# Slots 11 to 20 of a top-k attention and feed-forward kernel under one written timetable

## The chip, the cores and the metric

The kernel runs on one core of a Trainium2 chip. The metric is the device time of one execution in microseconds. Before the change the median of three runs is 1386.3 us (1385.4 to 1386.99).

## The reference

Queries, keys and values have 8 batches, 8 heads, 576 rows and a head dimension of 64. Each row of scores keeps its 32 largest entries, and the softmax over them weights the values. The heads of a row laid side by side give x (4608 rows of 512), which goes through a feed-forward block without biases.

```python
scores = scale * np.matmul(q, k.transpose(0, 1, 3, 2))
kth = np.partition(scores, -top_k, axis=-1)[..., -top_k:-top_k + 1]
scores = np.where(scores >= kth, scores, -1000000000.0)
attn = softmax(scores); x = rows of np.matmul(attn, v), heads side by side
h = x @ w_in
g = h * (1.0 / (1.0 + np.exp(-1.702 * h)))
return (g @ w_out).astype(np.float32)
```

All data are float32.

## The kernel before

The attention is cut into 144 slots, 18 to a batch. A slot holds 128 rows of scores for each of two heads: four tiles of 128 rows for each of four head pairs, and two slots for the last 64 rows of the batch, which pack two pairs each. The order on every engine is written out by hand (a manual schedule): each engine runs its queue in that order, and semaphores set by the tile framework hold an instruction until its operands and its buffer are ready.

A slot n goes through these steps. TensorE multiplies queries and keys (`scores`, L319, called two slots ahead) into one score tile of four PSUM banks. ScalarE copies it to SBUF (`copy_scores`, L334). VectorE pairs the two halves of a row into maxima and minima (`pair_up`, L343, done for slot n+1 within the search of slot n) and finds the 32 largest in four rounds of eight with `MAX8` and `MATCH_REPLACE8` (`topk`, L363; `find`, L1040, interleaves pairing, search and the inversion of the denominators of slot n-1). GpSimd makes the threshold and the shift (`bounds`, L388: `cut`, `low`). ScalarE masks (`mask`, L403) and takes exponentials with their sum (`exps`, L411); together they are `exponentials` (L397). GpSimd adds a small constant to the sum (`some`) and VectorE inverts it (`invert`, L422, `rden`). GpSimd multiplies (`normalize`, L439), ScalarE splits the float32 words into 16-bit halves (`split`, L475), SyncE writes them to DRAM and fetches them transposed (`turn_by_dma`, L483) into one of two `pt` buffers. TensorE multiplies them with the values (`values_at`, L537, for two slots at a time), and ScalarE brings the result into x (`x_of`, L595).

Four slots give one block of 128 rows of x. A block has four hidden units (`hidden`, L635: 16 or 32 matmuls with `w_in` into a PSUM bank), each followed by `tanh` on ScalarE, `gate` on GpSimd (L669), and a projection with `w_out` (`project`, L732). The first two blocks (`whole`) project straight. Later blocks use a product of seven quarter-size parts in place of eight: `combine` (L686) makes sums of the gated parts, and four sums of quarters of `w_out`, t1 to t4, are made once on GpSimd (`weight_sums`, L718, sixteen instructions run by `sum_weights`). Two PSUM banks, `both_banks` (L116, one tile), hold projections and, before slot 11, hidden units; after that, hidden units use the two rotating banks `ps_t`, which also hold q,k turns and attention outputs. When a block is done, `leave` or `leave_parts` copies its bank or banks out, and the parts are merged and written.

Slots 0 to 10 also round the weights and turn the attention by TensorE. Slots 11 and 12 are `first_pair` (L1055), slots 13 to 20 four calls of `filling_pair` (L1089), and from slot 21 `steady_pair` (L1149) runs to the end. The q,k pairs of batch 1 are turned by TensorE (`prepare_by_pe`, L297) at slots 13 to 15, batches 2 on by DMA (`prepare_by_dma`, L263; that of pair (2,0) at slot 21). In `filling_pair(n)` the values of slots n-3 and n-2 are taken late in slot n, between the scores of n+2 and n+3.

A loop serves two slots at once in the pairs, so one written order stands for both. In `first_pair` the output copies of the first block stand inside the second slot's exponentials:

```python
exponentials(n, leave_all)
```

Of the kernel before, what the change touches and what calls it, by code (L numbers as in the profile page):

```python
# [19 lines left out]
P = 128  # L20
# [13 lines left out]
def kernel(  # L34
# [81 lines left out]
    both_banks = ps_p.tile([P, 2, 512], F32, name="po")  # L116
# [53 lines left out]
    def stay_warm(count, of=ident[:]):  # L170

        none = both_banks[:, 1, :]
        for i in range(count):
            nc.tensor.matmul(none[:, 0:P], lhsT=of, rhs=of, start=True, stop=True)
# [122 lines left out]
    def prepare_by_pe(b, hp):  # L297
        for name in "qk":
            prepare_main(name, b, hp)
        second_part.append((b, hp))  # L300

    second_part = []
# [331 lines left out]

    def hidden(into=None):  # L635
        if not ready:
            return
        x = ready[0]
        fs, x.left = x.left[:G], x.left[G:]
        ph = ps_t.tile([P, G * P], F32, name="ph", tag="tp")[:] if into else both_banks[:, 0, :]  # L640
        for i, f in enumerate(fs):
            for c in range(CC):
                parts = 1 if x.whole else 2
                for y in range(parts):
                    rows = slice(y * P // parts, (y + 1) * P // parts)
                    nc.tensor.matmul(  # L646
                        ph[rows, i * P : (i + 1) * P],
                        lhsT=win[:, c, f * P + rows.start : f * P + rows.stop],
                        rhs=xs[:, x.place, c, :],
                        start=(c == 0),  # L650
                        stop=(c == CC - 1),
                    )
        to_gate.append((ph, fs, x))
        if not x.left:
            free.append(ready.pop(0).place)
# [62 lines left out]
    def weight_sums(to, x, y):  # L718

        def part(i, j):  # L720
            of = lambda name: half(name, i)[:, 2 * j : 2 * j + 2, :, :]
            nc.gpsimd.tensor_tensor(out=of(to), in0=of(x), in1=of(y), op=ALU.subtract)

        return [lambda i=i, j=j: part(i, j) for i in range(2) for j in range(2)]

# [6 lines left out]
    def project(put_off_leaving=False):  # L732

        g, sums, fs, x = to_project.pop(0)
        if x.whole:
            for i, f in enumerate(fs):
                nc.tensor.matmul(
                    both_banks[:, 1, :], lhsT=g[:, i * P : (i + 1) * P], rhs=wout[:, f, :],
                    start=(x.done == 0), stop=(x.done == FC - 1),
                )  # L740
                x.done += 1
        else:
            a11, a12, a22, s1, s2, s3, s4 = sums
# [4 lines left out]
            for bank, products in enumerate(banks):  # L748
                for i in range(2):
                    for r, (to, a, w) in enumerate(products):  # L750
                        for y in range(2):
                            nc.tensor.matmul(  # L752
                                both_banks[y * TAIL : (y + 1) * TAIL, bank, to * P : (to + 1) * P],
# [7 lines left out]
        def leave():  # L761
            ob = thp.tile([P, C], F32, name="ob", tag="th")
            nc.scalar.mul(out=ob[:], in_=both_banks[:, 1, :], mul=0.5 / RAISE**2)
            for i in range(2):
                nc.sync.dma_start(x.rows[:, i, :], ob[i * TAIL : (i + 1) * TAIL, :])

        def leave_parts():
            o = raws[:, 3, :].bitcast(F32).rearrange("p (r k) -> p r k", r=8)
            for bank, count in enumerate((4, 3)):
                nc.scalar.mul(  # L770
                    out=o[:, 4 * bank : 4 * bank + count, :].rearrange("p r k -> p (r k)"),
                    in_=both_banks[:, bank, 0 : count * P], mul=0.5 / RAISE**2,
# [16 lines left out]
        if x.done == FC:  # L789
            leaving.append(leave if x.whole else leave_parts)  # L790
            if x is blocks_seen[WHOLE - 1]:
                summing.extend(weight_sums("t3", "b22", "b12"))
# [43 lines left out]
    for b in range(1, B):  # L836
        for hp in range(NP):
            if b > 1:
                at(b * PER + FETCH[b % 2][hp], load_both, b, hp)
                at(b * PER + READY[b % 2][hp], prepare_by_dma, b, hp)  # L840
            else:
                at(b * PER + FETCH_1[hp], load_both, b, hp)
                at(b * PER + READY_1[hp], prepare_by_pe, b, hp)
# [18 lines left out]
    def prepare_first():  # L862
# [4 lines left out]
        ends = both_banks[:, 0, :].rearrange("p (g k) -> p g k", g=G)  # L867
# [60 lines left out]
    def slot(n):  # L928
# [85 lines left out]
        if idle:  # L1014
            stay_warm(8)
        hidden()

    def dues(n):

        preparing = prepare_by_dma, prepare_by_pe  # L1020
# [34 lines left out]
    def first_pair(n):  # L1055

        begin, prepare_some = dues(n)
        gate()
        bring_all()
        exponentials(n - 1)  # L1060
        find(n, 8)
        normalize(n - 1)
        split(n - 1)
        begin(0)
        turn_by_dma(n - 1)
        bounds(n)
        while unfinished:
            finish_one()
        scores(n + 2)
        copy_scores(n + 2)  # L1070
        leave_all()
        tanh(True)
        prepare_some()
        hidden(ps_t)
        project_one()
        tanh(True)
        exponentials(n, leave_all)
        find(n + 1, 8)
        scores(n + 3)
        copy_scores(n + 3)  # L1080
        normalize(n)
        split(n)
        begin(1)
        turn_by_dma(n)
        bounds(n + 1)
        gate()
        summing.extend(weight_sums("t1", "b12", "b11") + weight_sums("t2", "b22", "t1") + weight_sums("t4", "b21", "t2"))

    def filling_pair(n):  # L1089

        begin, prepare_some = dues(n)
        exponentials(n - 1)
        if n == STEADY:
            prepare_some()
        hidden(ps_t)
        if n > STEADY + 2:
            hidden(ps_t)
        tanh(True)
        if n > STEADY + 4:
            prepare_some()  # L1100
        combine()
        merge_some(2)
        find(n, 8)
        project_one()
        scores(n + 2)
        normalize(n - 1)
        split(n - 1)
        write_all()
        gate()
        begin(0)  # L1110
        turn_by_dma(n - 1)
        copy_scores(n + 2)
        bounds(n)
        prepare_some()
        mask(n)
        combine()
        merge_some(2)
        project_one()
        sum_weights(4)
        exps(n)  # L1120
        tanh(True)
        prepare_some()
# [8 lines left out]
        x_of(held, o)  # L1131
        for what in ends:
            copy_qk_ends(*what)
        find(n + 1, 8)
        scores(n + 3)
        copy_scores(n + 3)
        leave_all()
        normalize(n)
        split(n)
        write_all()  # L1140
        begin(1)
        turn_by_dma(n)
        while turns:
            turns.pop(0)()
        gate()
        bounds(n + 1)
        sum_weights(4)

    def steady_pair(n):  # L1149
# [8 lines left out]
        hidden(ps_t)  # L1158
        if n == STEADY + 8:
            tanh(True)  # L1160
            hidden(ps_t)
        leave_all()
        prepare_some()
# [3 lines left out]
        hidden(ps_t)  # L1167
        if live(n - 1):
# [53 lines left out]
    with tc.manual_schedule():  # L1222
# [41 lines left out]
```

## Time and profile before

| | |
|---|---|
| median of 3 runs | 1386.3 us (1385.4 to 1386.99) |
| profiled execution, first to last instruction | 1385.2 us |
| TensorE busy | 1345.7 us (97%) |
| VectorE busy | 1283.0 us (93%) |
| ScalarE busy | 1165.2 us (84%) |
| GpSimd busy | 963.8 us (70%) |
| mean granted TensorE clock | 0.987 |

The profile is of one execution. The profiled span lies 0.2 us below the fastest and 1.1 us below the median of the runs. Busy time is a sum over the span; PE stands for TensorE, DVE for VectorE, ACT for ScalarE, POOL for GpSimd, SP for SyncE. A number in brackets at the end of a timeline row is the idle time of that engine ahead of the instruction, with what ended it. Rows of equal instructions that follow each other are merged, and their first start and total length are shown. In rows of TensorE one float32 matmul appears as two records.

### The profile page before, as it was taken

What the parts mean: (1) busy time and instruction counts of PE and PEld (TensorE: products, weight loads), DVE (VectorE), ACT (ScalarE), POOL (GpSimd) and SP (SyncE); (2) the same over time, 40 slices, a digit from 0 to 9 for tenths busy, and PEclk for the clock granted to TensorE, in tenths of its full rate; (3) what the DMA queues carried; (4) which work ended last, traced back from release to release, by engine and by line L of the source; (5) the groups of instructions that cost most, each with busy time, mean ns of one, the idle gap of its engine ahead of it and who ended that gap; (6) DMA issues with size and microseconds to landing.
All of it is one profiled execution on the core that took longest, in us unless ns stands there. A gap on an engine that the chain in (4) does not pass through costs nothing. (4 is left out here: it accounts for less than half of the span.)

```text
span 1385.2 us, 54404 instructions
## 1 busy us (share of the span) xinstructions
PE 1345.7 (97%) x22560; PEld 1209.1 (87%) x22560; DVE 1283.0 (93%) x3392; ACT 1165.2 (84%) x1930; POOL 963.8 (70%) x1758
## 2 busy tenths in 40 slices
PE   7889889999999999999999999999999999999998
PEld 5676568899998999999999999999999999999997
DVE  7999889999999999999999999999999999999912
ACT  6888778999998998999998998889998998888831
POOL 3777586677777777777776777777777777777770
PEclk9899999999999999999999999999999999999999
DMA  8552556988889776977798678887898878855640
GB/s 231 161 151 67 128 150 160 212 200 199 199 208 206 177 184 174 237 198 196 194 203 223 181 187 193 193 195 200 197 213 208 196 182 182 183 139 138 155 111 17
DMA packets 527223, 246.92 MB, mean 178 GB/s; under 512 B 458880, under 2 KB 505472, under 8 KB 526976
## 3 DMA queue, kind: packets, MB, share of 16 engines
q1 hardware_dynamic: 526544, 243.16, 71.7%
q8 instruction: 177, 2.90, 0.9%
q14 instruction: 70, 0.57, 0.1%
q10 hardware_dynamic: 432, 0.30, 0.1%
HBM read 46.01 MB, written 103.42 MB: 108 GB/s over the span
## 5 line engine op out<-in xcount | busy, mean ns | idle before, releaser
L375 DVE MAX8 top<-ranked 128x8 f32<-128x288 f32 (+1 forms) x1152 | 637.4, 595 | 0.0
L646 PEld LDWEIGHTS ph<-xT,win 128*64 128x64 f32 (+1 forms) x8736 | 479.7, 137 | 28.9 <-issue 25.0
L646 PE MATMUL ph<-xT,win 128*64 128x128 f32 (+1 forms) x8736 | 504.5, 273 | 0.0
L379 DVE MATCH_REPLACE8 ranked<-top,ranked 128x288 f32<-128x288 f32 (+1 forms) x864 | 462.3, 542 | 0.0
L479 ACT COPY sc<-pr 128x2304 uint16<-128x2304 uint16 x134 | 283.4, 2115 | 100.9 <-POOL pr L443 100.9
L443 POOL TENSOR_SCALAR pr<-pr,rden 128x576 f32<-128x576 f32 x268 | 198.0, 750 | 53.6 <-DVE rden L430 53.0
L417 ACT ACTIVATE pr<-sc,low 128x576 f32<-128x576 f32 x288 | 220.1, 771 | 0.0
L407 ACT ACTIVATE sc<-sc,cut 128x576 f32<-128x576 f32 x288 | 208.9, 781 | 5.6 <-POOL cut L393 5.6
L752 PE MATMUL po<-raws,h 128*64 128x128 f32 x2112 | 205.1, 273 | 0.2 <-POOL h L700 0.2
L752 PE MATMUL po<-wout,h 128*64 128x128 f32 x2112 | 205.2, 273 | 0.1
L349 DVE TENSOR_TENSOR ranked<-s_ps,sc 128x576 f32<-128x576 f32 x286 | 201.8, 747 | 0.3 <-ACT sc L339 0.3
L339 ACT COPY sc<-s_ps 128x576 f32<-128x576 f32 x286 | 168.5, 642 | 21.0 <-PE s_ps L328 13.6
L328 PE MATMUL s_ps<-qk_t 64*64 64x288 f32 x2304 | 177.5, 422 | 8.1 <-DVE ranked L349 7.7
L426 POOL TENSOR_SCALAR some<-den 128x2 f32<-128x2 f32 x132 | 29.3, 222 | 222.0 <-ACT pr L417 221.7
L675 POOL TENSOR_TENSOR th<-th,h 128x512 f32<-128x512 f32 x134 | 171.8, 1282 | 11.2
L752 PE MATMUL po<-wout,th 128*64 128x128 f32 x2176 | 165.2, 273 | 0.0
L752 PEld LDWEIGHTS po<-wout,h 128*64 128x64 f32 x2112 | 133.4, 137 | 0.6 <-POOL h L701 0.6
L752 PEld LDWEIGHTS po<-raws,h 128*64 128x64 f32 x2112 | 133.4, 137 | 0.5 <-POOL h L700 0.5
L328 PEld LDWEIGHTS s_ps<-qk_t 64*64 64x64 f32 x2304 | 76.1, 134 | 61.6 <-issue 14.4
L752 PEld LDWEIGHTS po<-wout,th 128*64 128x64 f32 x2176 | 127.7, 137 | 0.9 <-POOL low L394 0.4
L575 PE MATMUL o<-pt,v_l 128*64 128x128 f32 (+1 forms) x2240 | 124.8, 265 | 0.0
L575 PEld LDWEIGHTS o<-pt,v_l 128*64 128x64 f32 x2240 | 110.3, 137 | 10.1 <-issue 9.6
(111 smaller groups left out, 1631.3 us busy)
## 6 DMA issues: line engine op xcount, KB each, us to landing
rows<-sc SPq DMA_DIRECT2D x134, 576.0 KB, 3.8
qk_rows<-halves SPq DMA_DIRECT2D x24, 576.0 KB, 5.6
out_dram<-raws SPq DMA_DIRECT2D x68, 128.0 KB, 3.6
raws<-in_moe_w_in_dram SPq DMA_DIRECT2D x16, 512.0 KB, 4.9
raws<-in_moe_w_out_dram SPq DMA_DIRECT2D x16, 512.0 KB, 3.6
qk_l<-in_q_dram SPq DMA_DIRECT2D x28, 256.0 KB, 4.4
qk_l<-in_k_dram SPq DMA_DIRECT2D x28, 256.0 KB, 4.3
v_l<-in_v_dram SPq DMA_DIRECT2D x4, 1024.0 KB, 7.8
```

The lines of the kernel that those rows point to most:

```text
L328: nc.tensor.matmul(ps[rows, i, c, 0:HALF], lhsT=qT[b, hps[p]][on, cols], rhs=kT[b, hps[p]][on, FIRST[i] + c * HALF : FIRST[i] + (c + 1) * ...
L349: nc.vector.tensor_tensor(out=ranked[n][:, :, c, :], in0=a, in1=b, op=op)
L375: nc.vector.max(top[:, i, 8 * r : 8 * r + 8], of(r, i))
L379: nc.vector.match_replace(to, top[:, i, 8 * r : 8 * r + 8], of(r, i), LOWEST)
L407: nc.scalar.activation(sc[:, i, :], sc[:, i, :], AF.Prelu, bias=cut[:, i : i + 1], scale=SCALE, alpha=HUGE)
L417: nc.scalar.activation(pr[:, i * S : (i + 1) * S], sc[:, i, :], AF.Exp, bias=low[:, i : i + 1], accum_out=den[:, i : i + 1],)
L443: nc.gpsimd.tensor_scalar(pr[:, i, :], pr[:, i, :], st[n]["rden"][:, i : i + 1], 1.0, op0=ALU.mult, op1=ALU.mult)
L479: nc.scalar.copy(out=halves, in_=pr[:].bitcast(U16).rearrange("p (k h) -> p h k", h=2))
L575: nc.tensor.matmul(o[s][j * D : (j + 1) * D, cols], lhsT=lhsT, rhs=rhs, start=(s, j) not in halves[:k], stop=(s, j) not in halves[k + 1 :],)
L646: nc.tensor.matmul(ph[rows, i * P : (i + 1) * P], lhsT=win[:, c, f * P + rows.start : f * P + rows.stop], rhs=xs[:, x.place, c, :], start= ...
L675: nc.gpsimd.tensor_tensor(out=th[:], in0=th[:], in1=h, op=ALU.mult)
L752: nc.tensor.matmul(both_banks[y * TAIL : (y + 1) * TAIL, bank, to * P : (to + 1) * P], lhsT=a[:, i, :], rhs=weight(w, fs[i])[:, y, :], sta ...
```

## The change

The change rewrites slots 11 to 20. `first_pair` and `filling_pair` go, and `filling_slot` takes their place: every slot puts its exponentials first in ScalarE's queue, then the ScalarE and GpSimd work that stands beside the search, then the scores, their copy, normalization and split, then the work behind. One table in `filling` gives each slot its extra work. The two projections that wait from the whole blocks go to slots 12 to 15. The q,k pairs of batch 1 are turned at slots 10, 13, 15 and 16, and their copies to SBUF stand in the next slot. The values of slots 12 to 17 move one slot later (to 16, 18 and 20). The sixteen weight sums are queued at once after slot 11, ordered by unit (t1, t2, t4, t3 of the first quarter, then of the second), one to three beside or behind a slot. `both_banks` becomes two tiles of one bank each; the second whole block projects into bank 0, and hidden units of slots 14 to 16 use bank 1. The copy of pair (2,0) moves from slot 21 to slot 19. `steady_pair` is changed for slot 21 alone: its first hidden unit is taken behind the scores.

```diff
-    both_banks = ps_p.tile([P, 2, 512], F32, name="po")
+    both_banks = [ps_p.tile([P, 512], F32, name=f"po{i}") for i in range(2)]
...
+    def turn_qk(b, hp):
+        new_pair(b, hp)
         for name in "qk":
-            prepare_main(name, b, hp)
+            full = ps_t.tile([P, 512], F32, name="tp")
+            for t in range(NF):
+                nc.tensor.transpose(full[:, t * P : (t + 1) * P], of_load(name, loaded[b, hp])[:, t, :, :], ident[:])
+            turned.append(((qT if name == "q" else kT)[b, hp], 0 if name == "q" else TAIL, full))
         second_part.append((b, hp))
+    def copy_qk(count=2):
+        for _ in range(min(count, len(turned))):
+            dst, before, full = turned.pop(0)
+            nc.scalar.copy(out=dst[:, before : before + FULL], in_=full[:])
...
+            self.bank = 1 - len(blocks_seen) % 2
...
+    def free_bank():
+        return 0 if len(blocks_seen) <= WHOLE else 1
...
+    def all_weight_sums():
+        of = ("t1", "b12", "b11"), ("t2", "b22", "t1"), ("t4", "b21", "t2"), ("t3", "b22", "b12")
+        sums = [weight_sums(*names) for names in of]
+        return [sums[k][u] for u in range(4) for k in range(4)]
...
-    READY_1 = (-5, -5, -3, -3)
-    FETCH_1 = (-11, -6, -4, -4)
+    FETCH_1 = (-11, -6, -5, -4)
...
             project(n == SETTLED)
+        if n == SETTLED:
+            turn_qk(1, 0)
         hidden()
...
+    def filling_slot(n, beside, pool_ahead, behind, pool_behind, late=[]):
+        todo = later.pop(n, [])
+        due = [(fn, args) for fn, args in todo if fn is prepare_by_dma]
+        exponentials(n - 1)
+        for fn in beside:
+            fn()
+        for fn in pool_ahead:
+            fn()
+        find(n, 8)
+        for fn, args in todo:
+            if fn is load_v:
+                fn(*args)
+        scores(n + 2)
+        if n == PAIRED:
+            normalize(n - 1)
+            split(n - 1)
+            copy_scores(n + 2)
+        else:
+            copy_scores(n + 2)
+            normalize(n - 1)
+            split(n - 1)
+        write_all()
+        for fn, args in todo:
+            if fn not in (prepare_by_dma, load_v):
+                fn(*args)
+        turn_by_dma(n - 1)
+        while turns:
+            turns.pop(0)()
+        for fn in pool_behind:
+            fn()
+        bounds(n)
+        for fn in behind + late:
+            fn()
...
+        gate()
+        bring_all()
+        filling_slot(11, [copy_qk], [], [unit], [])
+        finish_all()
+        summing.extend(all_weight_sums())
+        filling_slot(12, [th], [sums(1)], [put, put, ends_in_turn], [])
+        filling_slot(13, [copy_ends, th, leave_all], [gate, sums(1)], [of_qk(1), put, held(13)], [sums(1)])
+        filling_slot(14, [copy_qk, bring], [gate, sums(1)], [put, hidden], [sums(1)])
+        filling_slot(15, [copy_ends, th], [sums(3)], [put, hidden, of_qk(2)], [gate])
+        filling_slot(16, [th, leave_all, copy_qk], [combine, sums(1)], [held(15), hidden, of_qk(3), ends_in_bank], [gate], [bring])
+        filling_slot(17, [copy_ends, copy_qk, th], [combine, sums(2)], [put, unit], [sums(1)])
+        filling_slot(18, [th], [sums(2)], [held(17), put], [gate])
+        filling_slot(19, [bring, lambda: prepare_by_dma(2, 0), th], [combine, sums(1)], [unit, put], [gate])
+        filling_slot(20, [held(19), th], [combine, sums(1)], [put, unit], [gate])
...
         if n == STEADY + 8:
+            brought.pop(0)()
+            leave_all()
             tanh(True)
+        else:
             hidden(ps_t)
-        leave_all()
-        prepare_some()
+            leave_all()
+            prepare_some()
         find(n, 8)
         if live(n + 2):
             scores(n + 2)
         hidden(ps_t)
+        if n == STEADY + 8:
+            hidden(ps_t)
...
-        first_pair(PAIRED)
-        for n in range(STEADY, N + 2, 2):
-            (filling_pair if n < STEADY + 8 else steady_pair)(n)
+        filling()
+        for n in range(STEADY + 8, N + 2, 2):
+            steady_pair(n)
```

In the table `put` is a projection, `unit` and `hidden` a hidden unit (into `ps_t` or into bank 1), `th` a tanh with its copy, `held(m)` the values of slots m-3 and m-2, `bring` their copy into x, and `of_qk` a turn of q and k.

More of the change, by code (lines that the diff above doesn't have):

```diff
@@ L742, in project @@
         else:
+            assert len(summing) <= 4 * (FC // G - 1 - x.done // G) or x is not blocks_seen[WHOLE]
             a11, a12, a22, s1, s2, s3, s4 = sums
@@ L1053, in project_one, with values_held @@
             project(True)
[L1055 to L1070, printed above, removed]
-        leave_all()
-        tanh(True)
-        prepare_some()
[L1074 to L1122, printed above, removed]
+    def values_held(n):
         held = n - 3, n - 2
@@ L1130, in filling_pair, with copy_ends @@
             values_at(m, o[:, i, :])
[L1131 to L1139, printed above, removed]
+        ends_turned.extend(ends)
+        return lambda: x_of(held, o)
+    ends_turned = []
+    def copy_ends():
+        while ends_turned:
+            copy_qk_ends(*ends_turned.pop(0))
+    def filling_slot(n, beside, pool_ahead, behind, pool_behind, late=[]):
[19 more added lines that the diff above has]
+            split(n - 1)
```

53 lines of the change are left out of this document (32 added, 21 removed).

## The prediction

> **What bounds the kernel now.** I began with the stretches of the run (window, length, then busy time and count of TensorE, its weight loads, VectorE, ScalarE, GpSimd, then granted clock, DMA share, GB/s).
>
> ```profile
> 136.00:200.00 64.00, 55.54 (x464) 37.63 (x464) 55.38 (x146) 47.31 (x88) 44.21 (x58) 0.89 0.52 129
> 200.00:250.00 50.00, 48.66 (x872) 43.12 (x868) 44.90 (x119) 42.57 (x70) 32.65 (x64) 1.00 0.69 179
> 250.00:300.00 50.00, 49.59 (x914) 45.75 (x916) 50.00 (x135) 44.44 (x73) 35.95 (x69) 1.00 0.91 199
> 300.00:1300.00 1000.00, 999.57 (x17899) 915.49 (x17895) 984.03 (x2604) 888.65 (x1439) 724.97 (x1385) 1.00 0.80 192
> ```
>
> From 250 us on TensorE is never free (999.57 of 1000): whatever brings its queue forward before that moves the end by as much, and nothing else does. In 136 to 250 both TensorE and VectorE have idle time, and the clock drops to 0.89. This is where slots 11 to 20 lie, as VectorE's timeline shows; L349 is the pairing of slot n+1, once in each slot.
>
> ```profile
> 136.67 1.40 DVE L349 TENSOR_TENSOR ranked<-s_ps,sc 128x576 f32<-128x576 f32 x2
> 151.75 0.17 DVE L428 TENSOR_SCALAR some<-den 128x2 f32<-128x2 f32 x1 [3.61 <-ACT pr L417]
> 190.90 0.17 DVE L430 RECIPROCAL rden<-some 128x2 f32<-128x2 f32 x1 [2.62 <-POOL some L426]
> 202.60 0.17 DVE L430 RECIPROCAL rden<-some 128x2 f32<-128x2 f32 x1 [2.97 <-POOL some L426]
> 236.68 1.41 DVE L349 TENSOR_TENSOR ranked<-s_ps,sc 128x576 f32<-128x576 f32 x2
> 264.06 1.40 DVE L349 TENSOR_TENSOR ranked<-s_ps,sc 128x576 f32<-128x576 f32 x2
> 281.32 1.41 DVE L349 TENSOR_TENSOR ranked<-s_ps,sc 128x576 f32<-128x576 f32 x2
> ```
>
> The first row pairs slot 12 (in slot 11), the fifth slot 22: ten slots took 236.68 - 136.67 = 100.0 us. The last two rows are two slots apart without a wait: 8.63 us a slot. Ten at that pace are 86.3, so 13.7 us were lost, mostly at the inversion of the denominators, which waits for ScalarE's exponentials (the bracket: idle time and what ended it). ScalarE's rows of slot 12 say why:
>
> ```profile
> 147.13 1.45 ACT L407 ACTIVATE sc<-sc,cut 128x576 f32<-128x576 f32 x2
> 149.61 0.60 ACT L763 ACTIVATE ob<-po 128x512 f32<-128x512 f32 x1 [1.03 <-PE po L737]
> 150.10 0.77 ACT L417 ACTIVATE pr<-sc,low 128x576 f32<-128x576 f32 x1
> ```
>
> Two units' tanh work stands ahead of the mask (147.13), and between mask and exponentials stands the output copy, which waits for a projection.
>
> **TensorE's account.** Its timeline, with the projection of a later block from the chain of waits (730.73):
>
> ```profile
> 141.17 1.20 PE L328 MATMUL s_ps<-qk_t 64*64 64x288 f32 x16
> 150.63 1.09 PE L233 MATMUL tp<-ident,qk_l 128*128 128x128 f32 x8
> 151.56 3.60 PE L737 MATMUL po<-wout,th 128*128 128x512 f32 x8
> 160.16 2.20 PE L328 MATMUL s_ps<-qk_t 64*64 64x288 f32 x16 [5.00 <-DVE ranked L349]
> 167.93 1.09 PE L546 MATMUL o<-pt,v_l 128*64 128x128 f32 x16
> 170.26 1.20 PE L328 MATMUL s_ps<-qk_t 64*64 64x288 f32 x16
> 171.40 3.71 PE L646 MATMUL ph<-xT,win 128*64 128x128 f32 x64
> 188.85 0.48 PE L237 MATMUL o<-ident,qk_l 128*128 128x128 f32 x1 [2.66 <-ACT qk_t L234]
> 189.47 1.97 PE L546 MATMUL o<-pt,v_l 128*64 128x128 f32 x16
> 231.34 1.20 PE L328 MATMUL s_ps<-qk_t 64*64 64x288 f32 x16
> 232.47 7.21 PE L646 MATMUL ph<-xT,win 128*64 128x128 f32 x128
> 248.06 1.20 PE L328 MATMUL s_ps<-qk_t 64*64 64x288 f32 x16 [0.56 <-DVE ranked L349]
> 250.41 0.45 PE L575 MATMUL o<-pt,v_e 64*64 64x64 f32 x12 [0.64 <-ACT h L665]
> 252.71 0.61 PE L752 MATMUL po<-wout,th 128*64 128x128 f32 x8
> 730.73 3.06 PE po L752 x56
> ```
>
> Scores advance the queue by 1.1 (170.26 to 171.40), a hidden unit by 3.6, a projection of a whole block by 3.6 and of a later block by 3.1, the turning of one q,k pair by 0.9 (150.63 to 151.56), a pair of values by 2.3 (167.93 to 170.26), ends of a pair by 0.1 to 0.2 (188.85 to 189.47 is two at half speed). From 141.17 (scores of slot 13) to 252.71 (values of 18 and 19 done) stand 12 scores (13.2), 9 units (32.4), 5 and 5 projections (18.0 and 15.5), 4 turns (3.6), ends (0.4) and 5 pairs of values (11.7, the last a little longer): 94.8 us of work in 111.5. The other 16.7 are idle time, half-speed stretches and small gaps: after the 5.00 gap the same scores take 2.20, and after the 2.66 gap values take 1.97 where 1.09 is usual.
>
> **The change, part by part.** Work is moved, not saved. By the order of the built program VectorE's order is unchanged through the filling; up to the values of 18 and 19 TensorE gets the same units, projections and turns, and only the turn of pair (1,0) goes ahead of the window, into slot 10 (0.9 us, so scores of 13 start at 142.1).
>
> *Exponentials lead ScalarE's queue.* What a slot allows comes from these rows:
>
> ```profile
> 122.97 0.22 POOL L393 TENSOR_SCALAR cut<-top 128x4 f32<-128x4 f32 x1 [3.37 <-DVE top L375]
> 123.23 1.44 ACT L407 ACTIVATE sc<-sc,cut 128x576 f32<-128x576 f32 x2 [0.43 <-POOL cut L393]
> 143.10 0.23 POOL L393 TENSOR_SCALAR cut<-top 128x4 f32<-128x4 f32 x1 [1.87 <-DVE top L375]
> 146.06 1.41 DVE L349 TENSOR_TENSOR ranked<-s_ps,sc 128x576 f32<-128x576 f32 x2
> 204.38 2.11 ACT L479 COPY sc<-pr 128x2304 uint16<-128x2304 uint16 x1 [1.16 <-POOL pr L443]
> 208.11 1.45 ACT L407 ACTIVATE sc<-sc,cut 128x576 f32<-128x576 f32 x2
> 211.42 0.17 DVE L430 RECIPROCAL rden<-some 128x2 f32<-128x2 f32 x1
> ```
>
> Cut to pairing is 2.96; the pairing and one 576-wide maximum follow (about 2.0), so the inversion is due 5.0 after the cut. Cut to mask is 0.26, mask to inversion 3.31 (208.11 to 211.42): 3.6. The slack is 1.4 us. The split starts 1.8 after its inversion (202.60 to 204.38) and takes 2.1, so it ends 8.9 after the cut, just as the next mask may start (8.63 + 0.26). The other ScalarE work goes beside the search, where 2.3 us are free; it is over-full in slots 16, 17 and 19 by my count, making the next mask 0.7 to 1.0 late, inside the slack. If that cover were gone, every microsecond beyond 1.4 would be one of VectorE's.
>
> *Weight sums unit by unit, and the copy of pair (2,0) in slot 19.*
>
> ```profile
> L722 POOL TENSOR_TENSOR raws<-wout,raws 128x512 f32<-128x512 f32 x8 | 9.9, 1275 | 0.0
> 240.34 2.15 ACT L268 COPY halves<-qk_l 128x2304 uint16<-128x2304 uint16 x1
> ```
>
> Before, four sums in a row (5 us) stood ahead of a denominator on GpSimd; now one to three. Slot 15 has three (3.8 us from 0.5 after the cut, in time for 4.5), slot 17 two behind a combination, which I put 0.2 us late. The copy's 2.1 us move from slot 21 into slot 19, beside the search; its two DMA writes follow the split's on SyncE, and nothing that is due soon stands behind them.
>
> *Waiting projections and held values.* With the pace of 8.63, TensorE's load by slot (scores first): 11: 4.7, 12: 8.4, 13: 8.1, 14: 8.3, 15: 9.2, 16: 8.2, 17: 7.8, 18: 6.5, 19: 7.8, 20: 10.1; then 15 to the values of 18 and 19. Sum 94.1. Scores may start when the pairing of the slot is over, 4.4 after the cut. Slot by slot, scores of 13 to 22 start at 142.1, 147.5, 156.3, 165.0, 173.5, 182.7, 192.2, 200.1, 208.4 and 218.6. TensorE waits 0.6 and 0.6 for pairings in 12 and 13, 0.2 in 15, 1.6 in 19, 1.2 in 17 for the q,k copies behind that slot's exponentials, and in 13 for the load of pair (1,1), queued on SyncE behind the split's write: 5.5 us lie between the split's end and that turn, and two loads must be issued and land in them, which by the landing times below (3.4 to 5.0 after issue) leaves a wait of 0 to 2; I take 0.7. Together 4.9. The values of 18 and 19 end at 142.1 + 94.1 + 4.9 = 241.1, where they end at 252.7 now: -11.6. VectorE's side agrees: it comes out some 12.5 us earlier, with two waits of 0.2 to 0.5 left.
>
> *The transposes on SyncE's queue* are what values wait for.
>
> ```profile
> rows<-sc SPq DMA_DIRECT2D x12, 576.0 KB, 3.4
> DMA to landing us min/median/max: 4.4/5.0/8.9
> ```
>
> A split's rows land 3.4 after issue and the transpose (second row, tile pt) 5.0 after its own: about 9 after the split. There are two pt buffers, so slot 14's transpose waits on SyncE until slot 16's values of 12 are done, with writes queued behind it; still, values of 15 land near 197 and are used at 202, those of 17 near 214 and 217.5. Tightest is slot 21: the write of slot 19's rows comes behind the load of v, which now waits for the values of 17, and the copy of scores 23 waits for that write: 0 to 2 us. TensorE is behind VectorE there, so I count 1.
>
> *Banks apart* adds a wait to each later block's second bank and to its copy out; before, ScalarE's rows there had none and TensorE did not stall, so 0, at most a few tenths.
>
> The sum against the span of 1385.2 is -11.6 + 1.0 = -10.6: span 1374.6. The median of the runs lies 1.1 above that span; I keep the distance: 1375.7.
>
> **The clock.** The row: after a gap of 2.66 us values ran at half speed. The new gaps are at most 1.6. [...] In rows: 200 to 250 has several gaps under 1 us and a clock of 1.00. [...]
>
> **The rivals.** (1) *ScalarE or GpSimd late beyond the slack* in slots 15 to 21. For: three over-full slots. Against: 1.4 us of slack each, and lateness does not add up across light slots. Price 1 us in three to seven slots: -8 to -4, time 1378.3 to 1382.3. (2) *Slower: values wait for their transposes.* In slots 16, 18 and 20 they stand ahead of all units on TensorE. If the chain on SyncE makes them s late, TensorE idles s and then runs at half speed, which cost about 2.1 behind the 2.66 gap (values 2.3 became 189.47 to about 194). Three times s + 2.1 exceeds 10.6 from s = 1.5, which needs transposes some 5 us later than the median; the slowest quoted is 3.9 later. With s = 3: +15.3 - 10.6, time 1391. (3) *The clock swings.* Half speed doubles a piece of work: from an eighth of the 94 us on it adds 12 and leaves nothing, 1387. Against: the waits on TensorE are fewer and shorter than now. (4) *It does not reach the end*: VectorE or a transfer holds steady slots, and the time stays 1385 to 1388. Against: 999.57 of 1000.
>
> **How the numbers follow.** Forecast -13.7 (VectorE never waits) to -8: 0.70. Rival 1: 0.14. Rival 2: 0.06, rival 3: 0.05, half of it between -8 and 0, rival 4: 0.05. About 0.2% (2.8 us) is what a measurement here can tell from no change. Faster: 0.70 + 0.14 + 0.03 = 0.87; same 0.05; slower 0.08. The range takes in the forecast and rival 1: 1386.3 - 13.7 = 1372.6 to 1382.3.
>
> **What would show it.** Right: the pairings of slots 12 and 22 are 86 to 88 us apart; no denominator waits over 1 us; the clock in 136 to 240 is near 1.00; TensorE's scores of 22 start near 218.6 and values of 18 and 19 end near 241. Wrong: a TensorE gap over 2 us ahead of values or of q,k turns, half-speed scores, or waits for ScalarE in slots 16 to 21; and idle time past 250 would say that the bound of the later slots is not TensorE.

## The result, and the profile after

The changed kernel takes 1378.6 us (median of 4 runs, 1378.13 to 1379.59) where the kernel before takes 1386.6 in the same session: a ratio of 0.9941, 95% interval 0.9927 to 0.9955, or 8.1 us less. Forecast were 10.6 less and 1375.7. The profiled executions span 1385.2 and 1377.8 us. A run's time is its span and 1.8 more (1379.59 for 1377.8), so 7.4 of the difference can be followed in the two traces. The experiments ran on several chips, on which the kernel before takes 1383.6 to 1386.4 us; each ratio below is to the kernel before on the same chip, and times of different chips are not compared.

The stretches of the run first, in the columns of the prediction's first fence (length, busy time of TensorE, its weight loads, VectorE, ScalarE, GpSimd, clock, DMA share, GB/s).

```profile
136.00:200.00 64.00, 59.69 (x601) 41.46 (x601) 61.83 (x166) 54.97 (x99) 47.01 (x67) 1.00 0.59 148
200.00:250.00 50.00, 47.13 (x896) 43.04 (x894) 44.69 (x117) 41.10 (x67) 34.12 (x63) 1.00 0.81 195
250.00:300.00 50.00, 50.00 (x888) 45.53 (x886) 50.00 (x137) 44.48 (x72) 36.91 (x70) 1.00 0.80 184
300.00:1300.00 1000.00, 998.75 (x17880) 914.59 (x17876) 983.83 (x2601) 886.55 (x1437) 725.61 (x1386) 1.00 0.79 192
```

In 136 to 200 TensorE is busy 4.2 us more and VectorE 6.5, and the clock is 1.00 instead of 0.89. In 200 to 250 nothing is won. VectorE's timeline of the changed kernel shows why (L360 is the pairing, L439 and L441 the inversion):

```profile
135.92 1.42 DVE L360 TENSOR_TENSOR ranked<-s_ps,sc 128x576 f32<-128x576 f32 x2
174.14 0.17 DVE L441 RECIPROCAL rden<-some 128x2 f32<-128x2 f32 x1 [0.42 <-POOL some L437]
192.50 0.17 DVE L441 RECIPROCAL rden<-some 128x2 f32<-128x2 f32 x1 [0.99 <-POOL some L437]
202.46 0.17 DVE L441 RECIPROCAL rden<-some 128x2 f32<-128x2 f32 x1 [1.23 <-POOL some L437]
226.38 1.42 DVE L360 TENSOR_TENSOR ranked<-s_ps,sc 128x576 f32<-128x576 f32 x2
238.22 1.42 DVE L360 TENSOR_TENSOR ranked<-s_ps,sc 128x576 f32<-128x576 f32 x2 [2.99 <-ACT sc L350]
241.37 0.17 DVE L441 RECIPROCAL rden<-some 128x2 f32<-128x2 f32 x1 [1.07 <-POOL some L437]
```

The pairings of slots 12 and 22 lie 226.38 - 135.92 = 90.5 us apart (100.0 before; 86 to 88 forecast). Of the waits of 2.6 to 3.6 for denominators, three of up to 1.23 are left up to slot 20. In slot 22's search a new one of 2.99 stands ahead of the pairing of scores 23, for ScalarE's copy of them. ScalarE's and SyncE's rows show what holds that copy:

```profile
226.58 0.59 SPq L210 DMA_DIRECT2D v_l<-in_v_dram  x1
227.22 1.49 SPq L221 DMA_DIRECT2D v_e<-in_v_dram  x2
228.76 1.14 SPq L492 DMA_DIRECT2D rows<-sc  x1
237.00 1.18 ACT L350 COPY sc<-s_ps 128x576 f32<-128x576 f32 x2 [4.63 <-DMA rows<-sc]
```

The write of the split's rows stands behind the load of v and lands at 237, 8.2 us after its issue; the copy needs the buffer it empties. TensorE's rows tell what all this means for the end:

```profile
141.56 1.20 PE L339 MATMUL s_ps<-qk_t 64*64 64x288 f32 x16
147.11 1.20 PE L339 MATMUL s_ps<-qk_t 64*64 64x288 f32 x16 [0.58 <-DVE ranked L360]
155.94 1.20 PE L339 MATMUL s_ps<-qk_t 64*64 64x288 f32 x16 [0.46 <-DVE ranked L360]
158.22 0.63 PE L303 MATMUL tp<-ident,raws 128*128 128x128 f32 x4 [0.49 <-DMA raws<-in_k_dram]
163.89 0.33 PE L237 MATMUL o<-ident,by 128*128 128x128 f32 x1 [1.61 <-ACT qk_t L311]
166.48 1.20 PE L339 MATMUL s_ps<-qk_t 64*64 64x288 f32 x16
192.55 0.65 PE L303 MATMUL tp<-ident,raws 128*128 128x128 f32 x4 [0.29 <-ACT qk_t L242]
194.82 1.19 PE L339 MATMUL s_ps<-qk_t 64*64 64x288 f32 x14 [0.89 <-ACT qk_t L311]
210.68 1.20 PE L339 MATMUL s_ps<-qk_t 64*64 64x288 f32 x16 [1.44 <-DVE ranked L360]
220.84 1.20 PE L339 MATMUL s_ps<-qk_t 64*64 64x288 f32 x16
242.04 0.33 PE L586 MATMUL o<-pt,v_e 64*64 64x64 f32 x4 [0.79 <-ACT h L681]
243.02 0.45 PE L586 MATMUL o<-pt,v_e 64*64 64x64 f32 x12 [0.64 <-ACT h L681]
245.31 0.61 PE L776 MATMUL po<-wout,th 128*64 128x128 f32 x8
```

The values of 18 and 19 end at 245.3, where they ended at 252.7: 7.4 earlier. From there to the last instruction are 1377.8 - 245.3 = 1132.5 us, before 1385.2 - 252.7 = 1132.5. So in this pair of traces the whole difference lies ahead of these values and goes to the end, and TensorE's queue sets the end, as the prediction had it. That the two stretches agree to the tenth is chance: over all traces of this document the same stretch is 1130.4 to 1135.7 us long, the longest in a second trace of the changed kernel. The 2.99 of VectorE cost TensorE 0.6: the wait of 0.79 for ScalarE was 0.18 before, and in that second trace, where VectorE waits 1.73, it is gone. The brackets add up to 7.2 us, the largest 1.61 at 163.89.

### The profile page after: what moved, and what is told of

It reads as the page before. It is cut to its first block, busy times and chain, and to the rows that moved or that the text cites. A ratio compares the mean times of both kernels' runs of the same rounds, so it can differ in the third digit from the quotient of the medians.

```text
span 1377.8 us, 54398 instructions
## 1 busy us (share of the span) xinstructions
PE 1341.2 (97%) x22560; PEld 1205.0 (87%) x22560; DVE 1286.0 (93%) x3392; ACT 1164.1 (84%) x1930; POOL 964.4 (70%) x1758
## 4 chain that ended last, share of the span: by engine, by line
PE 79%; DMA 3%; ACT 1%; issue 0%; POOL 0%; SPq 0%; DVE 0%; DVEq 0%; ACTq 0%; POOLq 0%
PE ph L662 32%; PE po L776 28%; PE o L586 10%; PE s_ps L339 9%; DMA pt<-rows 2%; DMA rows<-sc 1%; ACT pr L428 0%; ACT sc L418 0%; ACT sc L490 0%; ACT sc L350 0%; ACT halves L268 0%; ACT raws L794 0%; SPq L221 0%; POOL pr L454 0%; ACT h L681 0%
## 5 line engine op out<-in xcount | busy, mean ns | idle before, releaser
L662 PE MATMUL ph<-xT,win 128*64 128x128 f32 (+1 forms) x8544 | 493.8, 273 | 0.0
L662 PEld LDWEIGHTS ph<-xT,win 128*64 128x64 f32 (+1 forms) x8544 | 469.4, 137 | 27.6 <-issue 24.1
L360 DVE TENSOR_TENSOR ranked<-s_ps,sc 128x576 f32<-128x576 f32 x286 | 201.8, 747 | 3.8 <-ACT sc L350 3.8
L350 ACT COPY sc<-s_ps 128x576 f32<-128x576 f32 x286 | 168.5, 642 | 26.9 <-PE s_ps L339 14.4
```

What stands on the lines that cost most here:

```text
L360: nc.vector.tensor_tensor(out=ranked[n][:, :, c, :], in0=a, in1=b, op=op)
L662: nc.tensor.matmul(ph[rows, i * P : (i + 1) * P], lhsT=win[:, c, f * P + rows.start : f * P + rows.stop], rhs=xs[:, x.place, c, :], start= ...
```

## Which part brings it

**The changed kernel, run once more** beside the experiments below, as a measure of how well runs and marks repeat.

> The changed kernel as it is, beside the two kernels that follow, on one chip: 0.994 of the time before, and the values of 18 and 19 end 103 to 104 us behind the start of the scores of slot 13, as in its first profile.

1379.1 us, ratio 0.9946 (0.9932 to 0.9960). The time repeats; the values of 18 and 19 end 102.5 us behind the start of scores 13 (243.8 less 141.3), a little outside the 103 to 104 expected. Between traces I compare a mark inside TensorE's queue: the start of scores 29 less that of scores 13. It is 153.5 us before, 145.7 after, and 144.4 in this repeat; the kernel before with its banks apart (below), which takes the same time as the kernel before, has 151.9. So a difference between two traces under some 1.6 us is not told apart from chance. Past 300 us TensorE is idle 0.2 to 2.9 us of 1000 in seven of the traces, whatever was edited, so a span alone is coarser still.

**Weight sums four in a row, all else as changed.**

```diff
-        return [sums[k][u] for u in range(4) for k in range(4)]
+        return [sums[k][u] for k in range(4) for u in range(4)]
...
-        filling_slot(13, ..., [gate, sums(1)], ..., [sums(1)])
+        filling_slot(13, ..., [gate, sums(4)], ..., [])
```

and so in 14 to 16, with none in the other slots.

> The changed kernel, with the weight sums four in a row ahead of the denominators in slots 13 to 16 (all of t1, then t2, t4, t3), as the kernel before has them, in place of one to three in slots 12 to 20. My theory: GpSimd has 4.5 us after a slot's cut before its denominators are due. A gate or a combination and four sums take about 7 from 0.5 after the cut, so the denominators come 3 us late in slots 13, 14 and 16 and 1 us late in slot 15, VectorE waits about that long in each (3, 3, 1, 3), and since TensorE has few idle tenths to hide it, the end comes 6 to 9 us later: 1384 to 1388 if the changed kernel takes 1378.5. The rival: TensorE is behind VectorE in these slots, or later slots without sums give the time back, and less than 1 us is lost at the end though the waits are there.

1387.5 us, ratio 1.0005 (0.9992 to 1.0019): the whole gain is gone, some 8 to 9 us against the changed kernel's 0.9941 and 0.9946, as expected at the upper end. Timeline of this kernel (VectorE, GpSimd, TensorE):

```profile
159.20 0.17 DVE L441 RECIPROCAL rden<-some 128x2 f32<-128x2 f32 x1 [2.66 <-POOL some L437]
170.58 0.17 DVE L441 RECIPROCAL rden<-some 128x2 f32<-128x2 f32 x1 [2.64 <-POOL some L437]
180.06 0.17 DVE L441 RECIPROCAL rden<-some 128x2 f32<-128x2 f32 x1 [0.76 <-POOL some L437]
191.44 0.17 DVE L441 RECIPROCAL rden<-some 128x2 f32<-128x2 f32 x1 [2.64 <-POOL some L437]
153.89 4.97 POOL L739 TENSOR_TENSOR raws<-wout 128x512 f32<-128x512 f32 x4
166.62 0.48 PE L237 MATMUL o<-ident,by 128*128 128x128 f32 x1 [4.29 <-ACT qk_t L311]
```

Expected were waits of 3, 3, 1 and 3; they are 2.66, 2.64, 0.76 and 2.64. TensorE's wait for the bank at 163.89 has grown from 1.61 to 4.29, since the copy that frees it stands behind exponentials that are later by VectorE's wait, and the values behind that gap take nearly twice as long (1.97 for 1.09). The rival falls.

**ScalarE's other work ahead of the exponentials, all else as changed.**

```diff
     def filling_slot(n, beside, pool_ahead, behind, pool_behind, late=[]):
...
-        exponentials(n - 1)
         for fn in beside:
             fn()
+        exponentials(n - 1)
```

> The changed kernel, with the ScalarE work that stands beside the search (tanh, bank copies, outputs of the values) queued ahead of the slot's exponentials instead of behind them, in all of slots 11 to 20; nothing else moves. My theory: VectorE waits for the denominators by this work's length less the 1.4 us of slack: about 0.4 in slot 13, 1 in 15, 1.5 in 16 and in 17, 2 in 19; TensorE's wait of 1.6 in slot 13 for the bank with the turned q shrinks by 1 or more, since its copy comes earlier. Net 3 to 7 us above the changed kernel. The rival: TensorE is the later engine, and the bank copies that come earlier on ScalarE give back what VectorE waits, so that the time is within 1 us of the changed kernel.

1404.1 us, ratio 1.0140 (1.0119 to 1.0161): by the ratios 19 slower than before and some 27 above the changed kernel, where 3 to 7 were expected. The direction held, the price did not. Two slots of its timeline:

```profile
160.31 0.21 ACT L240 COPY qk_t<-tp 128x64 f32<-128x64 f32 x1 [5.98 <-PE tp L237]
165.40 0.17 DVE L441 RECIPROCAL rden<-some 128x2 f32<-128x2 f32 x1 [6.90 <-POOL some L437]
198.04 0.60 ACT L678 ACTIVATE th<-po 128x512 f32<-128x512 f32 x1 [6.02 <-PE po L662]
203.76 0.17 DVE L441 RECIPROCAL rden<-some 128x2 f32<-128x2 f32 x1 [7.13 <-POOL some L437]
```

I had priced the work that stands ahead by its length. But this work waits itself, for TensorE: 5.98 for turned ends, 6.02 for a hidden unit. With the exponentials behind it, that wait becomes VectorE's (6.90, 7.13), and the next scores wait for VectorE. TensorE's gap ahead of the values taken in slot 13, which was expected to shrink from 1.61, grew to 3.94.

**Slot 12's exponentials ahead of the tanh work, in the kernel before.**

```diff
         copy_scores(n + 2)
+        exponentials(n)
         leave_all()
         tanh(True)
...
-        exponentials(n, leave_all)
+        leave_all()
```

> The kernel before with one part of the change: in slot 12 the exponentials stand ahead of the two units' tanh work and of the output copy on ScalarE. Theory (a late exponential holds VectorE, which holds the scores, which hold TensorE): VectorE's 3.61 us wait and TensorE's 5.00 us gap go, with the half-speed scores behind it; 3 to 5.5 us below the kernel before. Rival (only the whole timetable pays; the later waits of 2.62 and 2.97 take back what is won): 0 to 1.5 us below.

1388.1 us, ratio 1.0013 (1.0003 to 1.0023): nothing won, if anything 2 us lost. The theory falls; the rival is right that what is won is taken back, but it had expected no loss. The 3.61 at 151.75 and the 5.00 at 160.16 of the kernel before are gone, and these stand in their place:

```profile
148.17 3.67 PE L737 MATMUL po<-wout,th 128*128 128x512 f32 x8 [2.24 <-ACT h L665]
160.85 0.70 PE L233 MATMUL tp<-ident,raws 128*128 128x128 f32 x4 [2.29 <-ACT qk_t L234]
151.88 0.60 ACT L763 ACTIVATE ob<-po 128x512 f32<-128x512 f32 x1 [2.88 <-PE po L737]
159.42 0.17 DVE L430 RECIPROCAL rden<-some 128x2 f32<-128x2 f32 x1 [2.67 <-POOL some L426]
```

The output copy (151.88) still waits for its projection, which waits for the tanh work that is later now (148.17). It no longer stands inside this slot's exponentials but ahead of the next slot's, and VectorE waits 2.67 one slot on.

**Weight sums unit by unit, alone, in the kernel before.**

```diff
-        summing.extend(weight_sums("t1", ...) + weight_sums("t2", ...) + weight_sums("t4", ...))
+        summing.extend(sums[k][u] for u in range(4) for k in range(4))
...
-        sum_weights(4)
+        sum_weights(2 if n > STEADY else 3)
...
-        sum_weights(4)
+        sum_weights(3)
```

> The kernel before, with one edit: the sixteen weight sums are queued unit by unit as in the changed kernel, and two or three of them stand where four stood (three in slots 13, 14, 16 and 18, two in 15 and 17); ScalarE's order stays as before. My theory: the waits for GpSimd's denominators shrink by the sums that are gone ahead of them, 1.26 us for one sum: 0.7 in slot 13, 0.7 in 14, 2.5 in 15, and nothing in 16, where the denominator waited for ScalarE and not for the sums. VectorE gains some 4 us, and the end, which follows TensorE, 2 to 4 us: 1382 to 1384 where the kernel before takes 1386. The rival: as with slot 12's exponentials, the other order on ScalarE takes it back, and the time is within 1 us of the kernel before, so that only both parts together bring the gain.

1384.6 us beside 1384.4, ratio 0.9999 (0.9990 to 1.0008). The time did not move, as the rival has it. Its mark of 150.5 lies 3.0 below the kernel before's 153.5, but only 1.4 below the 151.9 of the kernel with its banks apart, and so shows no gain either. The waits did move:

```profile
187.36 0.17 DVE L430 RECIPROCAL rden<-some 128x2 f32<-128x2 f32 x1 [0.40 <-POOL some L426]
198.40 0.17 DVE L430 RECIPROCAL rden<-some 128x2 f32<-128x2 f32 x1 [2.30 <-POOL some L426]
217.61 0.17 DVE L430 RECIPROCAL rden<-some 128x2 f32<-128x2 f32 x1 [1.55 <-POOL some L426]
236.74 0.17 DVE L430 RECIPROCAL rden<-some 128x2 f32<-128x2 f32 x1 [1.77 <-POOL some L426]
```

The denominators of slot 15 come 0.40 late instead of 2.62. Those of slot 16, where I had put the 2.97 down to ScalarE, are 2.30 late; but the kernel with its banks apart has 1.46 there, so this wait changes by more than that without any edit of the sums. Those of 18 and 20 wait 1.55 and 1.77 where they waited 0.57 and 1.09.

**Banks apart, alone, in the kernel before.** `both_banks` becomes two tiles, and nothing else.

> The kernel before, with its tile of two PSUM banks made into two tiles of one bank each, and nothing else changed. My theory: no wait in slots 11 to 20 hangs on the two banks being one tile, so 0, within 1 us of the kernel before. The rival: a projection into one bank waits for a copy out of the other, and taking that away is worth 1 to 3 us.

1384.9 us, ratio 0.9994 (0.9984 to 1.0004): 0 within the error, as the prediction took it.

Together: neither the one edit on ScalarE's order tried alone (slot 12) nor the one on GpSimd's brings a measurable gain, and taking either order out of the changed kernel costs all of its gain or more. The denominators need ScalarE's exponentials and GpSimd's `some`; a slot is as late as the later of the two. Two things were not tried alone in the kernel before: ScalarE's new order in all ten slots, and the new places of the projections, values and turns on TensorE. So the runs show that both orders are needed, not that they are enough.

## Where the missing 3 us are

**Values of 10 and 11 into the free bank.** In slot 13 they take the second of the two rotating banks while it still holds q of pair (1,1).

```diff
-    [of_qk(1), put, held(13)], [sums(1)])
+    [of_qk(1), put, held(13, both_banks[1])], [sums(1)])
```

> Changed kernel with one edit: the values of slots 10 and 11 (slot 13) go into bank 1, which is free there, in place of a rotating bank that holds the turned q of pair (1,1) until ScalarE copies it in slot 14. Theory (the missing microseconds are waits of TensorE for PSUM banks that ScalarE empties a slot later): the 1.61 us gap ahead of those values goes, the scores of slot 16 start 1.4 to 1.7 us earlier than at 166.5, ScalarE's lateness in slots 14 to 17 shrinks, and the values of 18 and 19 end 1.5 to 3 us earlier than at 245.3; time 1.5 to 3 us below the 1378.6 of the changed kernel. Rival (ScalarE's over-full slots 16, 17 and 19 make VectorE late, and VectorE sets the end of the filling): the gap goes, but VectorE's waits of 0.99 and 1.23 us in slots 17 and 18 stay; time within 0.5 us of 1378.6.

In this kernel the ends of pair (1,1), which lie in that bank too, are overwritten by slot 14's hidden unit before they are copied, so part of batch 1's keys is not the reference's; the work is the same. 1375.6 us, ratio 0.9938 (0.9926 to 0.9951): 3.0 below 1378.6, but on a chip where the kernel before is faster by as much; beside the changed kernel's 0.9941 and 0.9946 no gain is clear. A second one copies the ends in slot 14 (`[copy_qk, bring, copy_ends]`), which puts the data right.

> Changed kernel with the values of slots 10 and 11 in bank 1, as before, and with the ends of pair (1,1), which lie in the same bank, copied out in slot 14 ahead of the hidden unit that takes the bank (in the first form that unit overwrote them). Theory (bank waits of TensorE): as the first form's trace, the scores of slot 29 start 2 to 3.2 us earlier than in the changed kernel, and the time is 2 to 3.2 us below it on the same chip. Rival (the first form was faster because its order left the copy of the ends without a wait): 0 to 1 us below.

1377.5 us, ratio 0.9937 (0.9925 to 0.9949), beside 1379.1 for the changed kernel on that chip: 1.6 faster, with intervals that overlap, and between what theory (2 to 3.2) and rival (0 to 1) had. The timelines of the first and the second:

```profile
164.02 1.20 PE L339 MATMUL s_ps<-qk_t 64*64 64x288 f32 x16
```
```profile
158.15 0.63 PE L303 MATMUL tp<-ident,raws 128*128 128x128 f32 x4 [1.08 <-DMA raws<-in_k_dram]
164.58 1.20 PE L339 MATMUL s_ps<-qk_t 64*64 64x288 f32 x16
```

The wait of 1.61 is gone and scores 16 start at 164.0 and 164.6. Their start less that of scores 13 is 23.0 and 23.7 us, where it is 24.9 in both traces of the changed kernel: 1.9 and 1.2 earlier. VectorE's wait of 0.99 in slot 17 becomes 0.30 and 0.32, so it came from there; the 1.23 in slot 18 becomes 0.74 and 1.18. At the mark of scores 29 the two have 142.9 and 143.9, against 145.7 and 144.4, which alone is not safely more than chance.

**Ends of pair (1,2) copied in slot 16** instead of behind slot 17's exponentials, and, apart from it, **the load of v behind the split's write** in slots 11 to 20.

```diff
-    [combine, sums(1)], [held(15), hidden, of_qk(3), ends_in_bank], [gate], [bring])
+    [combine, sums(1)], [held(15), hidden, of_qk(3), ends_in_bank], [gate], [bring, copy_first_ends])
```
```diff
-        for fn, args in todo:
-            if fn is load_v:
-                fn(*args)
         scores(n + 2)
...
-            if fn not in (prepare_by_dma, load_v):
+            if fn is not prepare_by_dma:
```

> Changed kernel with one edit: the ends of pair (1,2) are copied late in slot 16 instead of in slot 17, so that the bank which the turned k of pair (1,3) takes is free in slot 16. Theory (bank waits): the turn of k no longer waits at 192.5, the ends of (1,3) and the scores of slot 19 follow 1 to 1.5 us earlier than at 194.8; mask of slot 16 some 0.35 us later; time 0.3 to 1.5 us below 1378.6. Rival (ScalarE full): the exponentials of slot 16 are later by what was added, the scores of slot 19 gain nothing; time 0 to 0.5 us above 1378.6.

> Changed kernel with one edit: the load of v for batch 1 is issued behind the write of slot 19's rows on SyncE instead of ahead of it. Theory (from slot 21 on TensorE alone sets the end): ScalarE's 4.63 us wait for that write goes and with it VectorE's waits of 2.99 and 1.07 us at slots 22 and 23, but the time falls only by what TensorE itself waits behind them (0.79 and 0.64 us at the values of 18 and 19): 0.3 to 1.4 us below 1378.6. Rival (VectorE's lateness there is carried to the end): 3 to 4 us below 1378.6.

Ratios 0.9951 (0.9937 to 0.9965) and 0.9944 (0.9932 to 0.9957), marks 145.5 and 145.3: alone, neither moves the time. Without the 0.29 the 0.89 ahead of scores 19 is still there. With the load behind, ScalarE's 4.63 and VectorE's 2.99 are gone, and so are TensorE's 0.79 and 0.64. But now a transpose holds SyncE for 7.25 with the next write behind it, and VectorE waits 2.39 later. In this one trace TensorE also stands 1.33 us in the middle of a hidden unit, for which the profile names no cause and which no other trace has there, so its mark may hide a gain of that size (SyncE, VectorE and TensorE of this kernel):

```profile
229.66 7.25 SPq L498 DMA_TRANSPOSE pt<-rows  x1
236.97 0.58 SPq L492 DMA_DIRECT2D rows<-sc  x1
248.27 0.17 DVE L441 RECIPROCAL rden<-some 128x2 f32<-128x2 f32 x1 [2.39 <-POOL some L437]
237.07 1.14 PE L662 MATMUL ph<-xT,win 128*64 128x128 f32 x17 [1.33 <-issue]
```

**All three**, first with the ends overwritten as above, then with them copied:

> Changed kernel with the three edits together (values of 10 and 11 in bank 1, ends of (1,2) copied in slot 16, v behind the write). Theory: the gains add, with TensorE's queue at the values of 18 and 19 some 3 to 5 us earlier than at 245.3; time 1373.5 to 1376. Rival (VectorE's pace is already the bound of the filling): no more than the best of the three alone, 1376.5 to 1378.

> Changed kernel with the three edits, the ends of (1,1) copied in slot 14. Theory: bank 1 gives 2.8, the ends 0.2 to 0.5, v behind the write 0.3 to 1.4 (less wait behind values); 3.3 to 4.7 us below the changed kernel on the same chip, ratio to before 0.9905 to 0.992. Rival (VectorE's pace bounds the filling): no more than bank 1 alone.

Ratios 0.9914 (0.9899 to 0.9929) and 0.9915 (0.9902 to 0.9928). The second takes 1375.0 us where the changed kernel on the same chip takes 1379.1 and the one before 1385.9: the version to keep, 10.9 faster than before. That is about what was forecast, but for a kernel without these three edits. The marks, 141.4 and 141.5 against 145.7 and 144.4, say the same: 3 to 4 us. Its VectorE waits between slots 12 and 20 are these two:

```profile
191.22 0.17 DVE L441 RECIPROCAL rden<-some 128x2 f32<-128x2 f32 x1 [0.30 <-POOL some L437]
200.19 0.17 DVE L441 RECIPROCAL rden<-some 128x2 f32<-128x2 f32 x1 [0.24 <-POOL some L437]
```

So edits of which none alone shows a clear gain bring 4.1 us together, 2.5 of them beyond the values in bank 1 alone. My reading is that the other two count only once the wait of slot 13 is gone, because TensorE is late for its own reason ahead of that; the two without the bank were not run, so this is not shown, and neither is which of the two carries more of the 2.5.

## Why the prediction was right, and where it was off

**The bound.** That TensorE carries the end was right: it is busy 998.75 of 1000 us, and what is won up to the values of 18 and 19 is there at the end. That this held to the tenth was luck, since the stretch behind them differs by some 5 us between traces.

**The signs.** Of the prediction's own signs, the clock (1.00 from 136 to 250) and the missing half-speed scores (1.20 each) came out. Four did not: the pairings are 90.5 apart and not 86 to 88; a denominator waits 1.23 where none was to wait over 1; scores of 22 start at 220.8 and the values of 18 and 19 end at 245.3, for 218.6 and 241; and TensorE waits for ScalarE in slot 17 (0.29 and 0.89, which the sum had as 1.2) and ahead of the values of 18 and 19 (0.79 and 0.64, which it had not). So the kind of gain was forecast rightly, and its size too high.

**ScalarE's order and the sums.** Right in kind: no wait of 2.6 to 3.6 up to slot 20, and the slack of 4.5 that I worked out for GpSimd gave the four waits of the sums in rows to 0.4 us. I had treated the two as parts that each take away waits of their own; the runs show that neither order can be missing. The bracket names only the later of two engines, and the prediction read it as the only one.

**TensorE's sum.** Forecast were a start at 142.1, 94.1 of work and 4.9 of waits, so 241.1; measured are 141.6, 96.6 and 7.2 (the brackets), so 245.3. Less the 1.0 that I counted for slot 21 on top, this is the whole miss: 4.2 - 1.0 = 3.2, between -10.6 and -7.4. Three steps were mis-sized:
- *Slot 13*, 0.7 for the load: the load cost 0.49, but 1.61 for the bank stands beside it. I had counted waits for banks and copies in slots 16 to 19, not that the values of 10 and 11 take the bank that still holds q of pair (1,1), whose copy stands behind slot 14's exponentials. It made scores 16 1.5 late (166.5 for 165.0), and they stay so. The two experiments take 1.2 to 1.9 us of it away at scores 16; in the second a wait of 1.08 for the load takes back a part.
- *Waits left out*: 0.79 and 0.64 for tanh's copies ahead of the values of 18 and 19. The second stood in a row that I quoted (250.41), and the sum passed over it.
- *Work*, 96.6 for 94.1. By the starts in TensorE's timeline, twelve scores take 14.4 for 13.2: 1.13 each where 1.1 was put in, and 1.8 for scores 19, of which fourteen of sixteen records came behind the wait of 0.89. Three turns take 3.3 for 2.7, since four transposes ahead of a wait count with their whole length (0.66) and not with what they advance the queue by (0.46). Four ends take 1.0 for 0.4. Hidden units and projections came out within 0.2 of what was put in.

**Slot 19**: 1.6 forecast, 1.44 found. **Slot 17**: 1.2 forecast, 0.29 and 0.89 found. **VectorE's waits**: two of 0.2 to 0.5 forecast, 0.42, 0.99 and 1.23 found. ScalarE's exponentials in slot 17 start late because scores 16 and all behind them are: with the values in bank 1 the 0.99 falls to 0.30. So the 1.4 of slack was used up by slot 13. With all three edits the waits are 0.30 and 0.24, as forecast.

**Slot 21**: a wait of 0 to 2 for the copy of scores 23, found 4.63; it cost the end 0.6 at most (0.79 for 0.18), where I counted 1.

**The rivals.** By its number the first (late engines, -8 to -4) fits as well as the forecast: the gain in the traces is 7.4, in the medians 8.1, at the border of the two. Its mechanism, ScalarE late beyond the slack, shows in slots 17, 18 and 21, but TensorE's largest wait is that for the bank in slot 13, which neither forecast nor rival had. The second did not happen: up to 250 us no values wait for their transposes. Nor did the third: the clock in 136 to 250 is 1.00 with gaps up to 1.61. The fourth falls, since the gain reaches the end.

## What to carry to other kernels

Where a result needs two engines one after the other, a wait names the later one (here GpSimd's `some` in the waits of 2.62 and 2.97); price an edit on it by what the other would then show, and try each edit alone and both together. Price a queue position by what the work ahead *waits for*, not by its length: a copy of 0.2 us that waited 6 us for a matmul made VectorE, two steps behind it, wait 6.9. In a written timetable follow each rotating buffer from its last reader, on whatever engine that reader is queued: the wait that was missed, 1.61 us, was a write waiting for a copy one slot on.

## What the runs showed of the hardware

How long TensorE's work took behind its gaps: after single gaps of 1.61 (163.89; values 1.09 as usual, granted clock 1.00 in 163.8 to 166.5) and 2.24 (148.17 of the kernel with slot 12's exponentials ahead; projection 3.67, where 3.60 is usual) it took its usual time. Behind gaps of 2.64 and 3.00 it took nearly twice that. Behind the 2.66 of the kernel before, the granted clock is 0.50 in 188.8 to 194.4. The first two rows are of the kernel before with its banks apart (values 1.98 for 1.09), the third of the one with the exponentials behind (scores 2.20 for 1.20):

```profile
188.09 0.47 PE L237 MATMUL o<-ident,qk_l 128*128 128x128 f32 x1 [2.64 <-ACT qk_t L234]
188.70 1.98 PE L546 MATMUL o<-pt,v_l 128*64 128x128 f32 x16
```
```profile
186.58 2.20 PE L339 MATMUL s_ps<-qk_t 64*64 64x288 f32 x16 [3.00 <-DVE ranked L360]
```

The length of the gap alone does not part the two. Earlier in the trace of the changed kernel a gap of 3.53 (91.83) is followed by turns of the attention that take 2.05, with a granted clock of 1.00 in 91.8 to 94.2, and one of 2.17 (102.56) by as many turns that take 2.88, with 0.68 in 102.5 to 105.4.

Slow work also stands behind gaps that follow each other closely. In the kernel with slot 12's exponentials ahead, gaps of 2.29 (160.85) and 1.62 (163.17) were followed by turns that took 1.09 for 0.66 (first row). In the kernel with the sums in rows, gaps of 0.91 (248.73) and 0.64 (249.71) were followed by slow values (second row, 3.27 for 2.09). The changed kernel's 0.79 and 0.64 in the same place were not:

```profile
163.17 1.09 PE L233 MATMUL tp<-ident,raws 128*128 128x128 f32 x4 [1.62 <-DMA raws<-in_k_dram]
```
```profile
250.09 3.27 PE L586 MATMUL o<-pt,v_l 128*64 128x64 f32 x64
```

So in these traces neither the longest gap nor the count of gaps tells whether the work behind is slow. Nor is the price the same each time: behind the 2.66 of the kernel before, the work is slow up to the scores at 193.94 (1.72 for 1.20), some 6 us; behind the 2.64 above, the second group of values, 2.8 us on, takes nearly its usual time again (1.13 for 1.04). These two traces are of kernels that take the same time.
